# A PSUM copy at the head of the feed-forward unit: ScalarE moves h to SBUF, and the cubic, the square and the absolute value read the copy

## The chip, the cores and the metric

The kernel runs on one core of a Trainium2 chip. The metric is the device time of one execution in microseconds; of several runs the median counts. Engines are named as in the profile: PE is TensorE, DVE is VectorE, ACT is ScalarE, POOL is GpSimd, SP is SyncE (it issues DMAs).

## What is computed

Attention whose heads are mixed before and after the softmax, followed by a feed-forward part whose activation is a rational function. Cut to what matters here:

```python
# attention: 4 batches, 12 heads, 448 rows, 64 wide
scores = einsum('bhij,hg->bgij', q @ k.T / 8, w_pre)
attn   = einsum('bhij,hg->bgij', softmax(scores), w_post)
x      = (attn @ v)            # reshaped to 1792 tokens x 768

# feed-forward: 768 -> 2048 -> 768
h  = x @ w_in
P  = a[0] + a[1]*h + a[2]*h**2 + a[3]*h**3
Q  = 1 + abs(b[0])*abs(h) + abs(b[1])*h**2
out = (P / (Q + 1e-6)) @ w_out
```

## The kernel before

The program has two parts. The attention part goes over 16 tiles of query rows and takes roughly the first 350 us. The feed-forward part is 64 **units** (`put_unit(u)`), each 128 columns of the hidden width (of 2048) by one batch of 448 tokens; four units in a row have the same batch, and 16 such turns make up the whole. A matrix product is made in three passes from a high and a low part of each operand, so that a unit costs TensorE 36 matmuls of 448 columns: 18 for h (`m1`, L879) and 18 for the output (`m2`, L969, six groups of three, one for each 128 output columns).

A unit goes as follows. `m1` writes h into a bank of the PSUM tile `ps_s`, of which there are two. ACT reads the bank three times: `cubic` (L892, tile `m`), `square` (L895, tile `sq`) and `mag` (L898, tile `ua`); `den` (L902) makes the linear part of Q from the square. DVE reads the bank twice more: `horner1` (L905) and `horner2` (L908) multiply `m` by h. `den2` (L912) adds up Q, ACT takes `log` (L915) and `seed` (L919, an exponential) for a first reciprocal, DVE refines it (`step1` L922, `step2` L925) and forms the quotient (`quot` L929). `hi` rounds the result to the high part (L236 where ACT does it, L238 where DVE does), and `lo` (L939, POOL or DVE) subtracts for the low part. Both go into the tile `g`, which `m2` reads. The outputs of a turn are added to the partial sums on DVE (L1006) and leave by DMA.

In the same stretch the weights of the next turns are converted from 64-bit to a high and a low 32-bit part, in pieces of 384 columns (L410 ACT, L415 POOL, L419, L424 and L430 DVE, L236 ACT, L446 POOL); they share all three engines with the units until about 715 us.

The order of instructions on each engine is not that of the code. Every operation is entered in a plan with a guessed duration, a due time `at` and the operations that it must wait for. `Plan.run` then goes through time and writes an order for each engine; where an operation may run on either of two engines (`hi`, `lo`, some copies out of PSUM), it takes the first that is free. A `Ring` of n buffers makes the taker of buffer k wait for all uses of buffer k - n. The use that frees a bank of `ps_s` is set at the end of the unit's vector chain:

```python
o = add("pe", 18 * 0.204, m1, [w_ld[fi][0:4], *x_ld[xn], R["ps_s"].take(), m1_op.get(u - 1)], at=at, extra=0.1)
...
d1 = add("dve", 0.54, horner1, [a1, a2, a3], at=at)
d2 = add("dve", 0.6, horner2, [d1], at=at)
...
R["ps_s"].uses[-1].extend([a1, a2, a3, d2])
```

So `m1` of unit u + 2 waits for `horner2` of unit u, among others.

Of the kernel before, what the change touches and what calls it, by code (L numbers as in the profile page):

```python
# [9 lines left out]
F32 = mybir.dt.float32  # L10
# [8 lines left out]
B, H, S, D = 4, 12, 448, 64  # L19
# [35 lines left out]
class Plan:  # L55
# [11 lines left out]
    def add(self, eng, dur, fn, deps=(), at=0.0, extra=0.0, since=0.0, after=(), mode=None, late=0.0):  # L67
        op = Op(eng, dur, fn, [d for d in deps if d is not None], at, extra, since, mode, late)
        op.behind = list(after)
        self.ops.append(op)  # L70
        return op
# [107 lines left out]
class Ring:  # L179
# [5 lines left out]
    def take(self):  # L185

        k = len(self.uses)
        self.uses.append([])
        return Slot(self, k)


def act(n, sb=True):
    return 0.08 + 1.0e-3 * n + (0.05 if sb else 0.0)
# [40 lines left out]
def move(nc, eng, o, i):  # L234
    if eng is nc.scalar:
        eng.copy(o, i)  # L236
    else:
        eng.tensor_copy(o, i)  # L238
# [3 lines left out]
def mixed_attention_then_rational_ffn(ctx: ExitStack, tc, q, k, v, w, wmix, mask, a, b2, out):  # L242
# [3 lines left out]
    nc = tc.nc  # L246
# [5 lines left out]
    add = plan.add  # L252
# [6 lines left out]
    base, after = ctx.enter_context(ExitStack()), ctx.enter_context(ExitStack())  # L259
    left, right, pairs2 = ExitStack(), ExitStack(), ExitStack()  # L260
    sb = {}
# [7 lines left out]
    def open_pools(stack, side, sizes):  # L269
        for name, bufs in sizes:  # L270
            sb[name] = stack.enter_context(
                tc.tile_pool(name=name, bufs=bufs, side=side, reuse_waits="tile"))
# [4 lines left out]
    R = {n: Ring(i) for n, i in (  # L277
        ("d", 2), ("e", 6), ("st", 6), ("q", 3), ("k", 2), ("cr", 3), ("cm", 2), ("cg", 1),
        ("co", 2), ("ps_s", 2), ("ps_t", 2), ("ps_u", 2), ("ps_a", 2), ("a", 2), ("v", 2), ("xs", 1), ("xo", 3),
        ("t", 2), ("g", 3), ("x", 1))}  # L280

    kpre = const.tile([128, 64], F32, name="kpre")
    kpost = const.tile([128, 2, BT], F32, name="kpost")
# [16 lines left out]
    NR = 3  # L300
# [50 lines left out]
    b1_op = add("act", 0.4, fit_ab, [ab_ld], at=90.0, late=4.0)  # L351
# [446 lines left out]
    for i in range(len(VIA) * NCV):  # L798
        g = first[1] + 6 + (first[NT - 1] - first[1] - 3) * i // (len(VIA) * NCV)
# [2 lines left out]

    def begin():
        right.close()
        open_pools(after, "right", (("wr", NR), ("t", 2)))

    def rest():
        left.close()
# [57 lines left out]
    def put_unit(u):  # L866
# [3 lines left out]
        at = END1 + UNIT * u  # L870
        box = {}
# [13 lines left out]
        def new(nm):  # L885
            box[nm] = sb["t"].tile([128, S], F32, tag=nm, name=nm)
            return box[nm]

        def cubic():
            if u == 0:  # L890
                nc.scalar.preload_act_table_set("natural_log_exp_and_others")
            nc.scalar.activation(new("m"), box["h"], AF.Identity, scale=a_sb[:, 3:4], bias=a_sb[:, 2:3])  # L892

        def square():
# [46 lines left out]
        o = add("pe", 18 * 0.204, m1, [w_ld[fi][0:4], *x_ld[xn], R["ps_s"].take(), m1_op.get(u - 1)], at=at, extra=0.1)  # L941
        m1_op[u] = o
        w_use[fi].append(o)
        x_use[xn].append(o)
        t_free = R["t"].take()
        a1 = add("act", 0.61 if u else 1.9, cubic, [o, t_free, b1_op], at=at)
        a2 = add("act", act(S, False), square, [o, t_free], at=at)
        a3 = add("act", 0.52, mag, [o, t_free], at=at)
        a4 = add("act", 0.65, den, [a2, t_free, b1_op], at=at)
        d1 = add("dve", 0.54, horner1, [a1, a2, a3], at=at)  # L950
        d2 = add("dve", 0.6, horner2, [d1], at=at)
        d3 = add("dve", 0.54, den2, [a3, a4], at=at)
        a6 = add("act", act(S), log, [d3], at=at)
        a7 = add("act", act(S), seed, [a6, t_free], at=at)
        d4 = add("dve", 0.54, step1, [a7], at=at)
        d4 = add("dve", 0.6, step2, [d4], at=at)
        d5 = add("dve", 0.6, quot, [d4, d2], at=at)
        R["ps_s"].uses[-1].extend([a1, a2, a3, d2])
        a5 = add(copies(S, on=ON["g_hi"]), 0, hi, [d5, R["g"].take(), op_rest], at=at)
        d6 = add(subs(S, on=ON["g_lo"]), 0, lo, [a5], at=at)  # L960
        R["t"].uses[-1].append(d6)
# [149 lines left out]
```

## Time and profile before

| | |
|---|---|
| median of 3 runs | 845.81 us (841.18 to 846.6) |
| the profiled execution | 839.4 us |
| its span, first to last instruction | 837.6 us |
| granted TensorE clock, mean | 0.994 |
| busy share of the span | PE 96%, DVE 82%, ACT 59%, POOL 41% |

The profiled execution is one execution, and lies 1.8 us above its own span and 6.4 us under the median of the runs. Times inside it are read as differences and then set against the median. A busy PE is not PE at its peak, but idle time of PE is time in which it had nothing that it was allowed to start.

### The profile page before, as it was taken

The page shows a single profiled execution, that of the slowest core. Times are in us where ns is not written, and L with a number is a line of the kernel's source. Part 1 is how long each engine was busy: PE and PEld are TensorE (multiplying, and loading weights), DVE is VectorE, ACT ScalarE, POOL GpSimd, SP SyncE. Part 2 cuts the span into 40 slices and gives each one's busy share as a digit, 9 for nine tenths or more (in the row PEclk, how much of TensorE's full clock was granted, in tenths as well). Part 3 has the DMA queues.
Part 4 walks back from the last instruction along what each step waited for, and adds up shares of the span by engine and source line. Part 5 has one row for each costly group of instructions (what it writes and reads, how often), then busy time and mean ns, then how long its engine had stood idle before and what let it go on. Part 6 is the DMA issues. An engine that isn't in the chain of part 4 may idle for free.

```text
span 837.6 us, 23295 instructions
## 1 busy us (share of the span) xinstructions
PE 802.3 (96%) x9360; PEld 597.7 (71%) x9360; DVE 684.7 (82%) x1177; ACT 493.8 (59%) x1079; POOL 339.4 (41%) x464
## 2 busy tenths in 40 slices
PE   5789999999999999999999999999999999999998
PEld 1244454454444454589989899998999998999997
DVE  5677788788788888889988988999998999866665
ACT  2456667556565566576676665666566566445542
POOL 2224444343444343734555434465445455212111
PEclk8999999999999999999999999999999999999999
DMA  6678788677886775985633255753485544166314
GB/s 203 197 207 225 241 269 250 198 222 239 261 243 202 241 233 157 341 292 204 230 123 100 80 194 209 280 186 101 148 309 186 219 151 151 61 225 242 114 62 154
DMA packets 75355, 166.46 MB, mean 199 GB/s; under 512 B 12944, under 2 KB 52720, under 8 KB 74096
## 3 DMA queue, kind: packets, MB, share of 16 engines
q1 hardware_dynamic: 74648, 164.01, 59.1%
q8 instruction: 74, 1.21, 0.6%
q10 hardware_dynamic: 600, 0.97, 0.4%
q14 instruction: 33, 0.27, 0.1%
HBM read 88.50 MB, written 37.75 MB: 151 GB/s over the span
## 4 chain that ended last, share of the span: by engine, by line
PE 57%; DVE 16%; ACT 3%; issue 3%; POOL 2%; DMA 1%; SPq 0%; ACTq 0%; DVEq 0%; POOLq 0%
PE ps_s L879 19%; PE ps_u L969 6%; PE ps_a L969 6%; PE ps_t L969 6%; PE ps_a L640 5%; PE ps_s L496 5%; PE ps_t L565 3%; PE ps_u L705 3%; PE ps_u L565 2%; PE ps_t L705 2%; DVE cg L424 2%; DVE ua L925 2%; DVE cm L430 1%; DVE nm L571 1%; DVE ua L929 1%
## 5 line engine op out<-in xcount | busy, mean ns | idle before, releaser
L415 POOL TENSOR_SCALAR cm<-cm 128x384 f32<-128x384 f32 x64 | 103.3, 1616 | 46.6 <-ACT cm L410 46.3
L656 DVE STREAM_TRANSPOSE aa<-ps_a 128x448 f32<-128x448 f32 (+1 forms) x184 | 107.7, 617 | 13.7 <-PE ps_a L640 13.2
L939 POOL TENSOR_TENSOR g<-ua,g 128x448 fp32r<-128x448 f32 x47 | 57.8, 1230 | 138.8 <-ACT g L236 73.6
L600 POOL TENSOR_SCALAR krs<-kpost,rr 128x64 f32<-128x64 f32 x180 | 81.5, 466 | 74.3 <-DVE rr L591 54.0
L879 PE MATMUL ps_s<-xs,w 128*128 128x448 f32 x504 | 107.5, 366 | 2.9 <-DVE m L908 2.9
L879 PE MATMUL ps_s<-d,w 128*128 128x448 f32 x504 | 107.5, 366 | 1.3 <-DVE m L908 1.3
L496 PE MATMUL ps_s<-kk,q 64*64 64x448 f32 x720 | 94.4, 553 | 9.2 <-DMA kk<-in_k 5.0
L879 PEld LDWEIGHTS ps_s<-xs,w 128*128 128x128 f32 x504 | 94.4, 188 | 11.9 <-DVE m L908 4.0
L879 PEld LDWEIGHTS ps_s<-d,w 128*128 128x128 f32 x504 | 94.3, 188 | 10.3 <-DVE m L908 1.7
L236 ACT COPY st<-ps_s 120x448 f32<-120x448 f32 (+1 forms) x121 | 60.6, 533 | 68.1 <-PE ps_s L496 33.6
L640 PEld LDWEIGHTS ps_a<-e,krs 64*32 64x32 f32 x2880 | 45.2, 106 | 74.5 <-issue 34.4
L640 PE MATMUL ps_a<-e,krs 64*32 64x224 f32 x2880 | 93.6, 358 | 1.2 <-DVE aa L656 0.6
L446 POOL TENSOR_TENSOR w<-cm,w 128x384 fp32r<-128x384 f32 x48 | 54.7, 1140 | 87.7 <-ACT w L236 87.7
L892 ACT ACTIVATE m<-ps_s,a_sb 128x448 f32<-128x448 f32 x64 | 46.1, 720 | 69.5 <-PE ps_s L879 69.2
L969 PE MATMUL ps_u<-g,w 128*128 128x448 f32 x336 | 83.9, 366 | 0.0
L969 PE MATMUL ps_a<-g,w 128*128 128x448 f32 x336 | 83.8, 366 | 0.0
L969 PE MATMUL ps_t<-g,w 128*128 128x448 f32 x336 | 83.4, 366 | 0.0
L580 ACT ACTIVATE e<-ps_t,nm 128x448 f32<-128x448 f32 x92 | 57.7, 634 | 26.5 <-DVE nm L571 22.4
L587 POOL TENSOR_SCALAR sm<-sm 128x2 f32<-128x2 f32 (+1 forms) x92 | 20.9, 227 | 123.5 <-ACT e L580 121.4
L915 ACT ACTIVATE ua<-sq 128x448 f32<-128x448 f32 x64 | 37.0, 579 | 55.5 <-DVE sq L912 55.1
L580 ACT ACTIVATE e<-ps_u,nm 128x448 f32<-128x448 f32 x88 | 55.2, 634 | 24.0 <-DVE nm L571 20.4
L969 PEld LDWEIGHTS ps_t<-g,w 128*128 128x128 f32 x336 | 63.0, 188 | 5.6 <-DVE g L939 0.3
(89 smaller groups left out, 1516.5 us busy)
## 6 DMA issues: line engine op xcount, KB each, us to landing
d<-st SPq DMA_DIRECT2D x144, 210.0 KB
cr<-in_w SPq DMA_DIRECT2D x64, 384.0 KB
o_scr<-o SPq DMA_DIRECT2D x36, 448.0 KB
o<-o_scr SPq DMA_DIRECT2D x36, 448.0 KB
d<-x_scr SPq DMA_DIRECT2D x5, 2688.0 KB
xs<-x_scr SPq DMA_DIRECT2D x4, 2688.0 KB
d<-st SPq DMA_DIRECT2D x42, 157.5 KB
x_scr<-xs SPq DMA_DIRECT2D x12, 540.0 KB
```

The costliest lines, as they stand in the source:

```text
L236: eng.copy(o, i)
L415: nc.gpsimd.tensor_scalar(out=m, in0=m, scalar1=F64_MIN, scalar2=F64_MAX, op0=ALU.max, op1=ALU.min)
L446: eng.tensor_sub(t[:, 1, :], box["m"].bitcast(F32), t[:, 0, :].bitcast(F32))
L496: nc.tensor.matmul(box["s"][hh][i0:i1, 0:S], lhsT=Q[T][d, pr, i0:i1], rhs=K[b][d, pr, :], start=True, stop=True)
L580: nc.scalar.activation(e, box[r]["t"][:, 0:S], AF.Exp, bias=box[0]["nm"][:, r:r + 1], accum_out=box[0]["sm"][:, r:r + 1])
L600: eng.tensor_scalar_mul(box[r]["kr"], kpost, rr)
L640: nc.tensor.matmul(banks[c]["p"][q_:q_ + BT, JH * r:JH * (r + 1)], lhsT=box[r]["kr"][p, m_, :], rhs=box[r]["e"][p, JH * jh:JH * (jh + 1)], ...
L656: nc.vector.transpose(o, src)
L879: nc.tensor.matmul(h[:, 0:S], lhsT=W[fi][:, wi, kk * 128:(kk + 1) * 128], rhs=x[:, kk // 3, xj, kk % 3, :], start=(n == 0), stop=(n == 3 * ...
L892: nc.scalar.activation(new("m"), box["h"], AF.Identity, scale=a_sb[:, 3:4], bias=a_sb[:, 2:3])
L939: eng.tensor_sub(g[:, 1, :], box["rc"], g[:, 0, :].bitcast(F32))
L969: nc.tensor.matmul(O[key][:, 0:S], lhsT=W[fi][:, wi, DM + m * 128:DM + (m + 1) * 128], rhs=box["g"][:, gi, :], start=(f == 0 and n == 0), ...
```

## The change

ACT copies h out of the PSUM bank as the first step of a unit (`take`, L894, which calls the helper `move`, so that its rows have L236 or are told by their tile `h`). The copy lies in a new SBUF tile `h` with a single buffer. `cubic`, `square`, `mag`, `horner1` and `horner2` read the copy. The bank of `ps_s` is free once `take` is done; the single buffer `h` is free once `square`, `mag` and `horner2` of the unit are done, so that `take` of unit u + 1 waits for `horner2` of unit u. The plan's guessed costs for the three ACT operations are adjusted a little.

```diff
@@ rings and pools
-        ("t", 2), ("g", 3), ("x", 1))}
+        ("t", 2), ("h", 1), ("g", 3), ("x", 1))}
...
-        open_pools(after, "right", (("wr", NR), ("t", 2)))
+        open_pools(after, "right", (("wr", NR), ("t", 2), ("h", 1)))
@@ put_unit
-        def cubic():
+        def take():
             if u == 0:
                 nc.scalar.preload_act_table_set("natural_log_exp_and_others")
+            h = box["h"]
+            box["h"] = sb["h"].tile([128, S], F32, tag="h", name="h")
+            move(nc, nc.scalar, box["h"], h)
+
+        def cubic():
             nc.scalar.activation(new("m"), box["h"], AF.Identity, scale=a_sb[:, 3:4], bias=a_sb[:, 2:3])
...
-        a1 = add("act", 0.61 if u else 1.9, cubic, [o, t_free, b1_op], at=at)
-        a2 = add("act", act(S, False), square, [o, t_free], at=at)
-        a3 = add("act", 0.52, mag, [o, t_free], at=at)
+        a0 = add("act", act(S, False) + (0.0 if u else 1.3), take, [o, R["h"].take()], at=at)
+        R["ps_s"].uses[-1].append(a0)
+        a1 = add("act", 0.61, cubic, [a0, t_free, b1_op], at=at)
+        a2 = add("act", act(S), square, [a0, t_free], at=at)
+        a3 = add("act", 0.52, mag, [a0, t_free], at=at)
         a4 = add("act", 0.65, den, [a2, t_free, b1_op], at=at)
         d1 = add("dve", 0.54, horner1, [a1, a2, a3], at=at)
         d2 = add("dve", 0.6, horner2, [d1], at=at)
+        R["h"].uses[-1].extend([a2, a3, d2])
...
-        R["ps_s"].uses[-1].extend([a1, a2, a3, d2])
```

Since the plan sets the order, the change moves instructions, in the feed-forward part alone: the attention part up to the first units keeps its order. On PE the order is another one for the units 0 to 15, and the same as before from there on. On DVE and ACT rows move throughout. In the whole program DVE has 26 rounding casts of `hi` where it had 30, and 11 subtractions `lo` where it had 17 (the others are on ACT and POOL); of the units 16 to 48 alone these are 12 in place of 18, and 7 as before.

PE, around unit 12 (in the rows `ps_s` is written by `m1`, the other tiles by `m2`, x18 and x3 are matmuls in a row). Before, from the last piece of the outputs of unit 6 to the `m1` of unit 12, which is the third `m1` here:

```order
L969 MATMUL ps_a<-g,w_6258 128x448 x3
L969 MATMUL ps_a<-g,d 128x448 x3
L879 MATMUL ps_s<-d,w_6258 128x448 x18
L969 MATMUL ps_a<-g,d 128x448 x3
L879 MATMUL ps_s<-d 128x448 x18
L969 MATMUL ps_t<-g,w_6183 128x448 x3
L879 MATMUL ps_s<-xs,w_6183 128x448 x18
```

After, the `m1` of unit 11 and of unit 12 with what stands between them:

```order
L879 MATMUL ps_s<-d 128x448 x18
L976 MATMUL ps_u<-g,d 128x448 x3
L976 MATMUL ps_t<-g,w_6186 128x448 x3
L976 MATMUL ps_a<-g,d 128x448 x3
L976 MATMUL ps_t<-g,w_6186 128x448 x3
L976 MATMUL ps_a<-g,d 128x448 x3
L976 MATMUL ps_u<-g,w_6186 128x448 x3
L879 MATMUL ps_s<-xs,w_6186 128x448 x18
```

Before, three `m1` stand close together here, with one group of `m2` between each two of them; after, six groups of `m2` stand between two `m1`.

DVE, units 31 and 32 (`m` is written by `horner1`, TENSOR_TENSOR, and `horner2`; `sq` by `den2` and `step1`, `ua` by `step2` and `quot`; `cm` and `cg` are pieces of weights). Before, from `horner2` of unit 31:

```order
L908 SCALAR_TENSOR_TENSOR m<-m,a_sb,ps_s 128x448
L912 TENSOR_TENSOR sq<-sq,ua 128x448
L419 TENSOR_SCALAR cm<-cm 128x384
L424 SCALAR_TENSOR_TENSOR cg<-cr,cm 128x384
L905 TENSOR_TENSOR m<-m,ps_s 128x448
L430 SCALAR_TENSOR_TENSOR cm<-cr,cg 128x384
L908 SCALAR_TENSOR_TENSOR m<-m,a_sb,ps_s 128x448
L922 TENSOR_TENSOR sq<-sq,ua 128x448
L912 TENSOR_TENSOR sq<-sq,ua 128x448
L925 SCALAR_TENSOR_TENSOR ua<-sq,ua 128x448
L929 SCALAR_TENSOR_TENSOR ua<-m,a_sb,ua 128x448
```

After, from the same `horner2`:

```order
L913 SCALAR_TENSOR_TENSOR m<-m,a_sb,h 128x448
L419 TENSOR_SCALAR cm<-cm 128x384
L927 TENSOR_TENSOR sq<-sq,ua 128x448
L424 SCALAR_TENSOR_TENSOR cg<-cr,cm 128x384
L930 SCALAR_TENSOR_TENSOR ua<-sq,ua 128x448
L430 SCALAR_TENSOR_TENSOR cm<-cr,cg 128x384
L934 SCALAR_TENSOR_TENSOR ua<-m,a_sb,ua 128x448
L910 TENSOR_TENSOR m<-m,h 128x448
L917 TENSOR_TENSOR sq<-sq,ua 128x448
L913 SCALAR_TENSOR_TENSOR m<-m,a_sb,h 128x448
```

Before, `horner1` and `horner2` of unit 32 stand ahead of `step1`, `step2` and `quot` of unit 31; after, unit 31 is finished first.

ACT at the end of the program, units 62 and 63. Before, from `log` of unit 62:

```order
L915 ACTIVATE ua<-sq 128x448
L919 ACTIVATE ua<-ua 128x448
L892 ACTIVATE m<-ps_s,a_sb 128x448
L895 ACTIVATE sq<-ps_s 128x448
L898 ACTIVATE ua<-ps_s,b_sb 128x448
```

After, from the same `log`:

```order
L920 ACTIVATE ua<-sq 128x448
L236 COPY h<-ps_s 128x448
L924 ACTIVATE ua<-ua 128x448
L897 ACTIVATE m<-h,a_sb 128x448
L900 ACTIVATE sq<-h 128x448
L903 ACTIVATE ua<-h,b_sb 128x448
```

The copy of unit 63 stands between `log` and `seed` of unit 62, and `seed` waits behind it.

## Rows read from the trace of the kernel before

**Rows 1.** Busy time of each engine in five stretches of the span:

```profile
core 0: us, PE busy (x) PEld busy (x) DVE busy (x) ACT busy (x) POOL busy (x), PEclk, DMA share, GB/s
...
340.00:480.00 140.00, 137.35 (x1110) 119.62 (x1109) 124.79 (x215) 94.43 (x185) 69.46 (x70) 1.00 0.56 193
480.00:720.00 240.00, 237.62 (x1167) 218.75 (x1167) 219.52 (x358) 147.18 (x275) 118.66 (x89) 1.00 0.52 186
720.00:820.00 100.00, 100.00 (x495) 92.68 (x494) 67.72 (x114) 51.63 (x90) 15.58 (x14) 1.00 0.41 148
820.00:838.00 18.00, 13.66 (x68) 12.32 (x66) 8.61 (x15) 2.56 (x5) 2.49 (x2) 1.00 0.50 180
...
580.00:600.00 20.00, 18.66 (x92) 16.91 (x91) 19.46 (x31) 13.25 (x25) 11.20 (x8) 1.00 0.44 152
```

**Rows 2.** Waits of PE from 340 us on: total us, times, longest:

```profile
PE ps_s L879 <- DVE m L908: 4.2, 4, 1.6
```

**Rows 3.** Timeline at three of PE's four waits (brackets: idle before, releaser):

```profile
435.50 0.68 PE L879 MATMUL ps_s<-xs,w 128*128 128x448 f32 x2 [1.57 <-DVE m L908]
...
583.90 1.29 PE L879 MATMUL ps_s<-d,w 128*128 128x448 f32 x5 [1.33 <-DVE m L908]
...
702.59 1.69 PE L879 MATMUL ps_s<-xs,w 128*128 128x448 f32 x7 [1.05 <-DVE m L908]
```

**Rows 4.** ACT's and DVE's groups by form, 480 to 720 us:

```profile
L892 ACT ACTIVATE m<-ps_s,a_sb 128x448 f32<-128x448 f32 x33 | 23.8, 720 | 26.7 <-PE ps_s L879 26.7
L902 ACT ACTIVATE sq<-sq,c_sb,b_sb 128x448 f32<-128x448 f32 x33 | 25.2, 764 | 0.0
L895 ACT ACTIVATE sq<-ps_s 128x448 f32<-128x448 f32 x33 | 17.7, 535 | 0.0
L915 ACT ACTIVATE ua<-sq 128x448 f32<-128x448 f32 x32 | 18.5, 578 | 35.0 <-DVE sq L912 34.9
L908 DVE SCALAR_TENSOR_TENSOR m<-m,a_sb,ps_s 128x448 f32<-128x448 f32 x32 | 21.5, 671 | 0.1
L912 DVE TENSOR_TENSOR sq<-sq,ua 128x448 f32<-128x448 f32 x32 | 23.8, 745 | 0.0
L922 DVE TENSOR_TENSOR sq<-sq,ua 128x448 f32<-128x448 f32 x32 | 22.8, 714 | 7.0 <-ACT ua L919 6.7
L925 DVE SCALAR_TENSOR_TENSOR ua<-sq,ua 128x448 f32<-128x448 f32 x32 | 27.8, 870 | 0.6
L929 DVE SCALAR_TENSOR_TENSOR ua<-m,a_sb,ua 128x448 f32<-128x448 f32 x32 | 23.5, 734 | 0.6
L238 DVE CAST g<-ua 128x448 fp32r<-128x448 f32 x18 | 9.0, 500 | 1.8
```

**Rows 5.** Single lines, 480 to 720 us: ns shortest/median/longest:

```profile
L905 DVE TENSOR_TENSOR m<-m,ps_s x33: 605/611/622, 482.8 to 719.9; 128x448 f32<-128x448 f32 x33
L912 DVE TENSOR_TENSOR sq<-sq,ua x32: 607/616/1440, 483.4 to 712.3; 128x448 f32<-128x448 f32 x32
```

**Rows 6.** Timeline: `lo` on POOL, then the first `m2` of units 23, 31:

```profile
537.68 1.16 POOL L939 TENSOR_TENSOR g<-ua,g 128x448 fp32r<-128x448 f32 x1 [2.19 <-DVE g L238]
539.84 0.77 PE L969 MATMUL ps_t<-g,w 128*128 128x448 f32 x3
...
596.89 1.46 POOL L939 TENSOR_TENSOR g<-ua,g 128x448 fp32r<-128x448 f32 x1 [2.31 <-DVE g L238]
599.87 0.77 PE L969 MATMUL ps_t<-g,w 128*128 128x448 f32 x3
```

**Rows 7.** Timeline of the end, units 62 and 63:

```profile
818.51 0.73 ACT L892 ACTIVATE m<-ps_s,a_sb 128x448 f32<-128x448 f32 x1
...
822.60 0.58 ACT L915 ACTIVATE ua<-sq 128x448 f32<-128x448 f32 x1 [0.50 <-DVE sq L912]
...
826.55 1.15 POOL L939 TENSOR_TENSOR g<-ua,g 128x448 fp32r<-128x448 f32 x1 [2.96 <-DVE g L238]
...
828.03 0.77 PE L969 MATMUL ps_t<-g,w 128*128 128x448 f32 x3
```

## The prediction, written before the changed kernel was run

> **What bounds the kernel now.** I read the busy time by stretches first. From 340 us on the program is the feed-forward part, and PE is busy there all but a little: idle 2.65 us of 140, 2.38 of 240, none of 100, and 4.34 of the last 18 [rows 1]. The last of these is the closing sums and stores, which come behind the last matmul and which the change doesn't touch. So PE sets the time, at 36 matmuls a unit, and a change to the vector chain gains time only where PE waits for that chain. There is 2.65 + 2.38 = 5.0 us of idle time in front of the end, and nothing that this change does can gain more than that.
>
> The second view is what PE waits for. Of the 5.0 us, 4.2 us are four waits of `m1` for `horner2` [rows 2]: 1.57, 1.33 and 1.05 us [rows 3], which leaves 0.3 us for the fourth. It is the wait for a bank of `ps_s`: `m1` of unit u + 2 may start when `horner2` of unit u is done. That is the wait that the change loosens.
>
> The third view is the engine that is next. DVE is busy 219.5 of 240 us (91%) between 480 and 720 us, and 19.46 of 20 around the wait at 583.9 us [rows 1]. ACT has room there (147.2 of 240, 61%), and POOL (118.7, 49%). From 720 us on the weights are converted and DVE falls to 68 of 100. So the stretch where PE could be made to wait by a slower or later vector chain is 480 to 720 us, some 33 units.
>
> **What the change removes: the wait for the bank.** The bank is now free when the copy is done. The copy of unit u needs `m1` of u and `horner2` of u - 1, which comes some 7 us (a unit of PE's time: 240 us for 33 units [rows 1, 4]) before `horner2` of u. The three long waits were at most 1.57 us, so with 7 us of grace and 0.6 us of copy to pay, all four go. The gain is 4.2 us if nothing else is late in their place. The new order on PE for the units 0 to 15, which spreads the `m1` evenly, serves the same end: before, the 1.57 us wait came where the `m1` of units 10, 11 and 12 stood close together.
>
> **What it adds on ACT.** One copy a unit out of PSUM; the nearest row is `square`, which reads the same bank and writes SBUF: 0.535 us [rows 4]. The three readers change from PSUM to SBUF. `cubic` becomes what `den` is now, Identity with scale and bias out of SBUF: 0.764 in place of 0.720. `square` becomes what `log` is in size, 0.578 in place of 0.535 [rows 4], and `mag` I put up by the same 0.043. Together 0.535 + 0.044 + 2 x 0.043 = 0.67 us a unit, 22 us over 33 units; with six more rounding casts of some 0.57 us (0.535 and a little, estimated) it makes ACT 147 + 22 + 3.4 = 173 of 240 us, 72%. ACT hides it: it is idle while it waits for `m1` and for `den2` (26.7 and 34.9 us in [rows 4]). What isn't hidden is the length of a unit's chain, by the copy, a hand-over of 0.03 us and the slower reads: 0.70 us from `m1` to `horner1`.
>
> **What it does on DVE.** `horner1` and `horner2` now read two SBUF operands in place of one in PSUM and one in SBUF. That this may cost, two rows show. `horner1` never takes longer than 622 ns and never less than 605; `den2`, the same kind of operation with both operands in SBUF, takes 607 at least, 616 in the median, and up to 1440 [rows 5]. So there is no gain in the undisturbed duration, and a tail is added. The means of the four operations with both operands in SBUF lie over their floors: `den2` 745 and `step1` 714 against 612, `step2` 870 against 612, `quot` 734 against 671 [rows 4, 5], taking the floors from `horner1` and `horner2`. That is +0.13, +0.10, +0.26 and +0.06 us, 0.14 in the mean. The Trainium skill (SBUF — State Buffer, Who interferes with whom) says that a VectorE instruction with two SBUF inputs contends with a GpSimd instruction that reads SBUF, through a shared read port that the first to come holds. The spread in these rows agrees with that. For two operations I take 0.28 us a unit, with ends of 0.16 (2 x 0.08, the mean of the two smaller) and 0.39 (0.13 + 0.26): 33 units make 9.2 us, from 5.3 to 12.9. Against it, DVE has six casts fewer in the units 16 to 48, at 0.50 us [rows 4]: 3.0 us. Net +6.2 us, from 2.3 to 9.9, in a stretch where it had 240 - 219.5 = 20.5 us idle. DVE comes to 226 of 240, 94%.
>
> The Trainium skill (Perfetto Trace Analysis, Optimizing Scalar/DVE Operations) gives VectorE an access overhead of about 125 ns for PSUM against about 60 for SBUF, and by that the two operations would get cheaper by 0.13 us a unit, so that nothing is given back and the time is that of the full 4.2 us. Against it speak the shortest durations, 605 and 607 ns, which are the same [rows 5].
>
> **What is late next.** With the bank out of the way, the next thing that PE can wait for is `g`. In the stretch in question `lo` ends 1.0 us before the first `m2` of unit 23 starts (537.68 + 1.16 against 539.84) and 1.5 us before that of unit 31 (596.89 + 1.46 against 599.87) [rows 6]; three more units of the last place in their turn (35, 39, 47) are in the same position, and the other units of the stretch have more. Three things eat into it: the chain is 0.70 us longer, DVE is slower, and PE comes sooner by what it no longer waits (up to 2.4 us in this stretch). Against that the new order on DVE puts `step1`, `step2` and `quot` of unit 31 ahead of `horner1` and `horner2` of unit 32, at least 1.3 us (0.61 + 0.67 [rows 4, 5]) sooner. The two sides are about even. Ends: nothing is given back, or all that DVE gets more, 9.9 us, is passed on to PE. I take 1.2 us, half of the 2.4 us gained in this stretch, since 14 of DVE's 20.5 us of idle time are left to work a backlog off.
>
> **The end.** Unit 63 has 0.33 us to spare (826.55 + 1.15 = 827.70 against 828.03) [rows 7]. Worked through the new order with the prices above, one after the other: from 818.51 the copy 0.54, `seed` of unit 62 with 0.58 (as `log`), `cubic` 0.76, `square` 0.58 and `mag` 0.68 end at 821.65; then `horner1` and, now ahead of `horner2`, `den2` at 0.65 each, and a hand-over at either end, so that `log` starts at about 823.0 in place of 822.60 [rows 7]. That is 0.4 us, 0.1 more than the spare. Ends 0, where ACT's operations overlap, and 0.6 us (0.70 + 0.2 for DVE - 0.33), where the order gives nothing; I take 0.3.
>
> **The sum.** -4.2 + 1.2 + 0.3 = -2.7 us. Against the profiled execution of 839.4 us that is 836.7. That execution lies 6.4 us under the median, and no row says that the waits differ there; so against the median, 845.81 - 2.7 = 843.1, rounded to 843.0 us.
>
> **Rivals.** First, DVE takes it back and more. The place is 480 to 720 us. The price is two SBUF reads of 0.39 us a unit, 9.9 us net; it decides where the idle time of DVE is not where the backlog is, as around 583.9 us, where 0.54 of 20 us is idle [rows 1]. Then PE waits for `g` at the last units of the turns, and the sum is -4.2 + 9.9 + 0.3 = +6.0, 851.8 us; with the middle price, +6.2 in place of +9.9, it is +2.3, 848.1 us. For it speaks that DVE is at 97% there; against it, that PE had to wait only 2.4 us in 240 with this DVE.
>
> Second, the change doesn't free anything. The single buffer `h` makes `take` of unit u + 1 wait for `horner2` of u, and ACT executes in order: what stands behind `take` (`seed` of u in several places) waits too, and with it the chain that was to be freed. Where PE waited for `horner2`, it came up to 1.57 us after PE was free [rows 3]. Take 1.33 us, the wait at 583.9, as the delay of `seed`, and the longer chain of 0.70: with a spare of 1.0 us [rows 6], five units lose 5 x (1.33 + 0.70 - 1.0) = 5.2 us, and -4.2 + 5.2 + 0.3 = +1.3 makes 847.1 us. Against it: `horner2` stands within two DVE operations of `horner1` in nearly all units, and `log`, where it stands ahead of `take`, isn't held up.
>
> Third, all of the 4.2 us stay, and the end costs nothing: 841.6 us. It lies on the side of the forecast.
>
> **How the numbers follow.** The forecast with the third case, a gain of 1 to 4.2 us: 0.6. DVE takes it back: 0.25. Nothing is freed: 0.1. Something that I don't see: 0.05. The range takes in the third case and the first rival's middle price. The runs of before spread over 841.18 to 846.6, so 3 us are added at the low end and 2 at the high one: 838.5 to 850. One per cent, about what a measurement of this kernel can tell from no change, is 8.5 us. A gain of that size is more than the 5.0 us that PE idles, so 0.03; a loss of it needs more than the first rival's upper price, 0.06; within it 0.91.
>
> **What would show it.** PE's waits for `horner2` in front of `m1` are gone, all four. The copy takes about 0.54 us, `cubic` 0.76. `horner1` and `horner2` get a tail beyond 622 ns and means of some 0.7 to 0.85 us between 480 and 720 us, and DVE is busy 226 of 240 us. PE's waits there, if any, are for `g`, in the last units of turns, and sum to some 1 us. The prediction is wrong if PE's idle time between 340 and 820 us is over 5 us, or if the time changes by more than PE's idle time does, which would point to the attention part, whose order is the same.

## The result and the profile after

The changed kernel takes 854.39 us (median of 4 runs, 852.3 to 858.69), the kernel before in the same job 844.12 (4 runs, 841.18 to 846.6). The ratio is 1.0121, with a 95% interval of 1.0082 to 1.0159: the change costs some 10 us. 843.0 us was forecast, in a range up to 850; the time lies outside it, on the side of the first rival.

The profiled execution of after took 858.69 us, the longest of its four, and that of before, 839.4 us, lies below all of its runs. Part of the 19 us between the two is scatter ahead of the change: the first `m1` starts at 350.4 us in the one and 356.3 us in the other, though the attention part is the same, and in another execution of the kernel before it starts at 355.0 us. So the kernels are compared below by their medians and, of profiled executions, by the **feed-forward length**, from the start of the first `m1` to the end of the span: 487.2 us before, 487.1 in that other execution of it, 500.6 after. This length repeats far better than the whole.

Busy time by stretches of after, columns as in [rows 1]; the first row is the feed-forward part as a whole:

```profile
core 0: us, PE busy (x) PEld busy (x) DVE busy (x) ACT busy (x) POOL busy (x), PEclk, DMA share, GB/s
356.30:856.90 500.60, 485.96 (x2616) 439.81 (x2612) 420.98 (x668) 330.29 (x608) 225.85 (x159) 0.99 0.49 172
...
356.00:486.00 130.00, 125.63 (x884) 110.80 (x877) 107.07 (x174) 93.74 (x180) 68.86 (x54) 1.00 0.52 177
486.00:739.00 253.00, 246.35 (x1183) 223.80 (x1182) 231.84 (x363) 175.75 (x324) 138.29 (x92) 0.99 0.50 178
739.00:838.00 99.00, 99.00 (x490) 91.75 (x489) 71.33 (x116) 56.11 (x98) 16.54 (x14) 1.00 0.41 149
580.00:600.00 20.00, 16.55 (x72) 14.45 (x71) 18.25 (x29) 12.39 (x23) 10.48 (x9) 0.91 0.28 92
700.00:720.00 20.00, 17.54 (x78) 15.43 (x77) 18.21 (x29) 13.63 (x27) 10.67 (x8) 0.91 0.33 109
```

The same whole of before:

```profile
350.30:837.60 487.30, 479.12 (x2620) 438.06 (x2612) 410.73 (x680) 290.36 (x538) 198.67 (x155) 1.00 0.50 176
```

PE's idle time in the feed-forward part is 500.60 - 485.96 = 14.6 us where it was 487.30 - 479.12 = 8.2, so +6.5. Its busy time, for the same matmuls, is 486.0 in place of 479.1, so +6.8. The 13.3 us are in these two. Idle time is lost up to 739 us, while the weights are still converted (4.4 + 6.7 us against 5.0 in [rows 1]); behind that PE never stops for 99 us, as before. Of the longer busy time, most lies in two stretches of 20 us in which the granted clock has a mean of 0.91: PE is busy 16.55 and 17.54 us there with 72 and 78 matmuls, which at the rate of [rows 1] (495 in 100 us) would take 14.5 and 15.8, so 3.8 us more. Another part stands beside the waits, as time that the view counts as busy. An example, at a clock of 1.00:

```profile
520.51 0.37 PE L976 MATMUL ps_t<-g,w 128*128 128x448 f32 x1
521.29 0.67 PE L976 MATMUL ps_t<-g,w 128*128 128x448 f32 x2 [0.42 <-DVE g L944]
521.80 0.78 PE L976 MATMUL ps_u<-g,w 128*128 128x448 f32 x3
```

The first group of three takes 1.29 us from its start to that of the next, where groups start some 0.62 apart undisturbed; 0.42 of the 0.67 us between count as idle, 0.25 as busy. (Estimate: eight waits outside the two stretches, against four before, make some 1 us.) That leaves some 2 of the 6.8 us that no row here shares out.

What PE waits for in after, 340 us on (total us, times, longest):

```profile
PE ps_t L976 <- POOL g L944: 5.9, 8, 1.0
PE ps_t L976 <- ACT g L236: 3.9, 2, 2.4
...
PE ps_t L976 <- DVE g L238: 0.6, 1, 0.6
...
PE ps_t L976 <- DVE g L944: 0.4, 1, 0.4
```

The four waits for `horner2` in [rows 2] are gone, all of them. In their place are twelve waits for `g`, 10.8 us. The result of the vector chain comes too late for `m2`, at the first of its six groups. Counted by `quot`, 7.0 of the 10.8 us fall on the last units of turns (11, 19, 27 and 43), the rest on the units 10, 12 to 14 and 22; 3.3 us lie before 480 us.

DVE, POOL and ACT by form, 499 to 739 us of after (columns as in [rows 4]; `den2` is L917, `step1` L927, `step2` L930, `quot` L934):

```profile
L913 DVE SCALAR_TENSOR_TENSOR m<-m,a_sb,h 128x448 f32<-128x448 f32 x32 | 33.5, 1047 | 0.0
L917 DVE TENSOR_TENSOR sq<-sq,ua 128x448 f32<-128x448 f32 x32 | 24.8, 776 | 1.2 <-ACT sq L907 1.1
L927 DVE TENSOR_TENSOR sq<-sq,ua 128x448 f32<-128x448 f32 x32 | 24.6, 770 | 11.2 <-ACT ua L924 11.2
L930 DVE SCALAR_TENSOR_TENSOR ua<-sq,ua 128x448 f32<-128x448 f32 x32 | 22.6, 707 | 0.7
L934 DVE SCALAR_TENSOR_TENSOR ua<-m,a_sb,ua 128x448 f32<-128x448 f32 x32 | 22.4, 699 | 0.4
L910 DVE TENSOR_TENSOR m<-m,h 128x448 f32<-128x448 f32 x31 | 21.2, 682 | 0.7 <-ACT m L897 0.7
...
L446 POOL TENSOR_TENSOR w<-cm,w 128x384 fp32r<-128x384 f32 x27 | 37.7, 1400 | 26.5 <-ACT w L236 26.5
L944 POOL TENSOR_TENSOR g<-ua,g 128x448 fp32r<-128x448 f32 x25 | 36.5, 1461 | 49.2 <-DVE g L238 25.2 <-ACT g L236 24.0
...
L236 ACT COPY h<-ps_s 128x448 f32<-128x448 f32 x32 | 17.0, 530 | 17.2 <-DVE m L913 12.7 <-PE ps_s L879 2.4 <-DVE sq L927 1.7
```

`horner2` has a mean of 1,047 ns where it had 671 [rows 4], `horner1` 682 where its median was 611 [rows 5]. `step2` came down from 870 to 707: the six operations together go from 4.35 to 4.68 us a unit. POOL's subtractions are longer too: the low part of `g` took 1,229 ns in the mean in before (480 to 720 us), 1,461 now. The row of before, and that of the weights' low part in the second execution of before, 499 to 739 us:

```profile
L939 POOL TENSOR_TENSOR g<-ua,g 128x448 fp32r<-128x448 f32 x26 | 31.9, 1229 | 42.9 <-DVE g L238 24.6 <-ACT g L236 18.3
...
L446 POOL TENSOR_TENSOR w<-cm,w 128x384 fp32r<-128x384 f32 x26 | 29.3, 1128 | 48.6 <-ACT w L236 48.6
```

Single operations of after, same stretch (ns shortest/median/longest):

```profile
L913 DVE SCALAR_TENSOR_TENSOR m<-m,a_sb,h x32: 670/919/1595, 498.9 to 734.7; 128x448 f32<-128x448 f32 x32
...
L446 POOL TENSOR_TENSOR w<-cm,w x27: 1012/1398/2387, 507.1 to 733.7; 128x384 fp32r<-128x384 f32 x27
```

Sorted by what POOL does at the same time, over the whole feed-forward part of this trace: 39 of the 64 `horner2` overlap no subtraction of POOL and have a median of 675 ns; 22 overlap one by more than 0.3 us, and their median is 1,576.

The timeline around the longest wait of after:

```profile
568.47 1.32 POOL L446 TENSOR_TENSOR w<-cm,w 128x384 fp32r<-128x384 f32 x1 [1.04 <-ACT w L236]
...
568.84 1.43 DVE L913 SCALAR_TENSOR_TENSOR m<-m,a_sb,h 128x448 f32<-128x448 f32 x1
...
578.66 2.76 POOL L446 TENSOR_TENSOR w<-cm,w 128x384 fp32r<-128x384 f32 x2 [2.21 <-ACT w L236]
...
579.11 1.44 DVE L927 TENSOR_TENSOR sq<-sq,ua 128x448 f32<-128x448 f32 x1
...
580.59 1.32 DVE L930 SCALAR_TENSOR_TENSOR ua<-sq,ua 128x448 f32<-128x448 f32 x1
...
583.12 0.57 ACT L236 CAST g<-ua 128x448 fp32r<-128x448 f32 x1 [1.97 <-DVE ua L934]
...
583.74 0.47 PE L976 MATMUL ps_t<-g,w 128*128 128x448 f32 x1 [2.45 <-ACT g L236]
583.77 1.39 POOL L944 TENSOR_TENSOR g<-ua,g 128x448 fp32r<-128x448 f32 x1 [2.35 <-ACT g L236]
...
585.21 1.10 PE L976 MATMUL ps_t<-g,w 128*128 128x448 f32 x2 [1.00 <-POOL g L944]
...
586.11 1.32 PE L976 MATMUL ps_u<-g,w 128*128 128x448 f32 x3
...
587.23 1.32 PE L976 MATMUL ps_t<-g,w 128*128 128x448 f32 x3
...
589.11 0.78 PE L976 MATMUL ps_u<-g,w 128*128 128x448 f32 x3
589.73 0.78 PE L976 MATMUL ps_a<-g,w 128*128 128x448 f32 x3
```

In these rows the DVE operations on two SBUF tiles that lie beside a subtraction of POOL take about twice their time: `horner2` 1.43, `step1` 1.44, `step2` 1.32 us, against 0.6 to 0.7 undisturbed [rows 4, 5]; the subtractions take 1.3 to 1.4 us. PE stands still for 2.45 us and again for 1.00, and after that its groups of three matmuls start 1.12 us apart (586.11, 587.23) where they start 0.62 apart a little later (589.11, 589.73): the granted clock is at 1.2 GHz, the lower of its two levels, for a while, and at 2.4 GHz again afterwards. That is the 0.91 of the window above; two microseconds of it:

```profile
586.00:588.00 2.00, 2.00 (x7) 1.75 (x7) 1.97 (x5) 1.43 (x4) 0.79 (x1) 0.50 0.00 0
```

### The profile page after: what moved, and what is told of

Read it like the earlier page. It is cut to its first block, busy times and chain, and to the rows that moved or that the text cites. A ratio compares the mean times of both kernels' runs of the same rounds, so it can differ in the third digit from the quotient of the medians.

```text
span 856.9 us, 23412 instructions
## 1 busy us (share of the span) xinstructions
PE 815.0 (95%) x9360; PEld 600.2 (70%) x9360; DVE 695.7 (81%) x1165; ACT 534.0 (62%) x1149; POOL 366.6 (43%) x470
## 4 chain that ended last, share of the span: by engine, by line
PE 59%; DVE 20%; DMA 6%; ACT 6%; issue 5%; POOL 3%; SPq 1%; ACTq 0%; DVEq 0%; POOLq 0%
PE ps_s L879 16%; PE ps_s L496 7%; PE ps_a L640 6%; PE ps_u L976 6%; PE ps_t L976 6%; PE ps_a L976 5%; DMA d<-st 4%; PE ps_t L565 4%; PE ps_u L565 4%; ACT e L580 2%; PE ps_u L705 2%; PE ps_t L705 2%; DVE cg L424 2%; DVE ua L934 2%; DVE nm L571 2%
## 5 line engine op out<-in xcount | busy, mean ns | idle before, releaser
L944 POOL TENSOR_TENSOR g<-ua,g 128x448 fp32r<-128x448 f32 x53 | 73.8, 1393 | 160.4 <-DVE g L238 91.4
L415 POOL TENSOR_SCALAR cm<-cm 128x384 f32<-128x384 f32 x64 | 105.9, 1659 | 47.8 <-ACT cm L410 47.2
L236 ACT COPY st<-ps_s 120x448 f32<-120x448 f32 (+1 forms) x121 | 60.8, 533 | 76.3 <-PE ps_s L496 41.7
L496 PE MATMUL ps_s<-kk,q 64*64 64x448 f32 x720 | 97.0, 563 | 7.2 <-DMA kk<-in_k 5.2
L976 PE MATMUL ps_t<-g,w 128*128 128x448 f32 x336 | 88.3, 373 | 7.8 <-POOL g L944 4.2
L446 POOL TENSOR_TENSOR w<-cm,w 128x384 fp32r<-128x384 f32 x48 | 63.6, 1327 | 52.1 <-ACT w L236 52.1
L236 ACT COPY h<-ps_s 128x448 f32<-128x448 f32 x64 | 34.0, 532 | 65.4 <-PE ps_s L879 31.9
L927 DVE TENSOR_TENSOR sq<-sq,ua 128x448 f32<-128x448 f32 x64 | 47.3, 740 | 29.0 <-ACT ua L924 28.9
```

Of the source, the lines that this page charges most:

```text
L415: nc.gpsimd.tensor_scalar(out=m, in0=m, scalar1=F64_MIN, scalar2=F64_MAX, op0=ALU.max, op1=ALU.min)
L446: eng.tensor_sub(t[:, 1, :], box["m"].bitcast(F32), t[:, 0, :].bitcast(F32))
L496: nc.tensor.matmul(box["s"][hh][i0:i1, 0:S], lhsT=Q[T][d, pr, i0:i1], rhs=K[b][d, pr, :], start=True, stop=True)
L944: eng.tensor_sub(g[:, 1, :], box["rc"], g[:, 0, :].bitcast(F32))
L976: nc.tensor.matmul(O[key][:, 0:S], lhsT=W[fi][:, wi, DM + m * 128:DM + (m + 1) * 128], rhs=box["g"][:, gi, :], start=(f == 0 and n == 0), ...
```

## The experiments

The kernel before ran beside every group of them, at 843.0 to 844.9 us. "Feed-forward" is the feed-forward length of the profiled execution. (In e9, e10 and e12 POOL's results are left out, so that these three are compared with each other.)

| run | what is in it | median us | ratio to before, 95% | feed-forward us |
|---|---|---|---|---|
| before | | 844.12 | 1 | 487.2 |
| after | copy, five readers, 1 buffer, its own order | 854.39 | 1.008 to 1.016 | 500.6 |
| e1 | order of before; copy, five readers, 2 buffers | 857.25 | 1.008 to 1.022 | 499.0 |
| e2 | order of after, 2 buffers | 854.21 | 1.007 to 1.016 | 498.9 |
| e3 | order of after, horners read PSUM | 866.89 | 1.022 to 1.031 | 508.6 |
| e4 | 2 buffers known to the plan | 853.87 | 1.006 to 1.016 | 497.0 |
| e5 | order of before; copy, ACT's readers alone | 847.09 | 1.003 to 1.010 | 491.6 |
| e6 | order of before; only horners on SBUF | 851.01 | 1.006 to 1.012 | 495.2 |
| e7 | before once more | 843.20 | 0.996 to 1.000 | 487.1 |
| e8 | before, horners due earlier | 842.26 | 0.995 to 1.001 | 486.7 |
| e9 | before, POOL quiet | 836.97 | 0.991 to 0.996 | 481.3 |
| e10 | e1, POOL quiet | 839.28 | 0.993 to 0.998 | 481.3 |
| e12 | e5, POOL quiet | 839.23 | 0.993 to 0.998 | 481.7 |
| e11 | e4, measured DVE costs in the plan | 843.44 | 0.997 to 1.003 | 487.0 |
| e13 | after, measured DVE costs (1 buffer) | 849.48 | 1.004 to 1.013 | 495.1 |
| e14 | before, measured DVE costs | 839.51 | 0.993 to 0.999 | 482.4 |
| e15 | e4, guessed costs plus 5% | 850.50 | 1.006 to 1.012 | 491.2 |
| e16 | e4, measured costs less 10% | 843.46 | 1.000 to 1.005 | 487.9 |

**Is it the order, the buffer or the reads?** e1 keeps the plan and the order of before and puts the copy just ahead of `cubic`; the two buffers lie in a tile that is idle at that time.

```diff
+            h = box["h"]
+            box["h"] = sb["co"].tile([128, 2, CV], F32R, tag="co", name="h").rearrange("p a c -> p (a c)")[:, 0:S].bitcast(F32)
+            move(nc, nc.scalar, box["h"], h)
             nc.scalar.activation(new("m"), box["h"], AF.Identity, scale=a_sb[:, 3:4], bias=a_sb[:, 2:3])
```

> The plan and the order of the kernel before on every engine; the copy is issued just ahead of cubic, all five readers read it, and h has two buffers (in the space of the tile co, which is idle by then), so that nothing waits for horner2 but the second next copy. What is left of the change is the price of the operations: 0.7 us more on ACT's side of a unit's chain, and the two-SBUF reads of horner1 and horner2 on DVE. If the DVE reads are the cause, it loses most of the 10 us: 850 to 855 us. If the single buffer h or the new order is the cause, it comes out near the kernel before, 841 to 846 us, with PE's four waits for the bank gone or shorter.

It took 857.25 us. The loss is there without the new order. In the feed-forward part PE waits for `g` alone here, 10.5 us.

e2 is after with two buffers, the order untouched:

```diff
-            box["h"] = sb["h"].tile([128, S], F32, tag="h", name="h")
+            box["h"] = sb["co"].tile([128, 2, CV], F32R, tag="co", name="h").rearrange("p a c -> p (a c)")[:, 0:S].bitcast(F32)
```

> The order of the changed kernel on every engine, word for word, and all its reads; only h has two buffers, so that the copy of unit u + 1 no longer waits for horner2 of unit u. If the single buffer, by holding ACT's queue, is the cause: 843 to 847 us, and the 26 us in which the copy waited for horner2 between 356 and 740 us are gone. If the DVE reads or the new order are the cause: 851 to 855 us, as the changed kernel.

854.21 us. In after, `take` waits for `horner2` 30 times:

```profile
ACT h L236 <- DVE m L913: 29.2, 30, 3.0
```

In e2 that row is gone and the time is the same. e4 tells the plan of the second buffer (`("h", 2)` in the rings), which gives another order:

> The changed kernel with two buffers h, and the plan knows of them, so that the order is made anew. If the single buffer is the cause, 842 to 846 us, no slower than the run with two buffers in the unchanged order. If the DVE reads are, 850 to 855 us. If it is an order in which the first units run ahead and the outputs come late, anything between, and the first units tell.

853.87 us. With the plan's guessed costs a second buffer gives nothing back, in either order. (With other costs it does: e13 below.)

e3 is after with `horner1` and `horner2` reading the bank as before, the ACT readers on the copy:

```diff
-            h = box["h"]
+            h = box["hp"] = box["h"]
...
-            nc.vector.tensor_mul(box["m"], box["m"], box["h"])
+            nc.vector.tensor_mul(box["m"], box["m"], box["hp"])
...
-                out=box["m"], in0=box["m"], scalar=a_sb[:, 1:2], in1=box["h"], op0=ALU.add, op1=ALU.mult)
+                out=box["m"], in0=box["m"], scalar=a_sb[:, 1:2], in1=box["hp"], op0=ALU.add, op1=ALU.mult)
```

> The order of the changed kernel on every engine; horner1 and horner2 read the bank in PSUM as before, ACT's three readers read the copy. The copy's buffer is free after mag, so the wait of the copy for horner2 is gone too, and the bank is again held until horner2. If the DVE reads are the cause: 842 to 847 us, horner2 back from a mean of 1.05 us to 0.67. If the single buffer is: the same 842 to 847 us, but then the run with two buffers is as fast. If the order is: 851 to 855 us.

866.89 us, the slowest of all and above every value expected, with a new wait: in this order `m1` counts on a bank that is free early, and PE waits for `horner2` ten times, 15.9 us. It doesn't separate the reads from the order, so the next two go back to the order of before.

**The two halves alone.** e5 is e1 with the edit of e3: copy and ACT's readers, horners on PSUM.

> One half of the change in the order of the kernel before: ACT copies h just ahead of cubic, with two buffers, and cubic, square and mag read the copy; horner1 and horner2 read the bank in PSUM as before. It adds 0.7 us to the head of each unit's chain and to ACT, and nothing to DVE. If the DVE reads from SBUF are the cause: 844 to 848 us, since the longer head alone costs PE little. If ACT's added work and the longer chain are the cause: 851 to 857 us, as with all readers on the copy.

847.09 us, +3.6 over the before of its job (843.47) by the medians, 5.2 by the ratio of 1.0062. PE's waits are four for `horner2` as before, 6.4 us in place of 4.2: the chain is longer by the copy, and the bank comes free later. e1 and e5 differ only in where the two horners read h, and with it in when the bank is free: 857.25 against 847.09 us.

e6 has no copy; `horner1` and `horner2` multiply by a constant SBUF tile, so that the numerator of P/Q is not a function of h.

```diff
+    h_sb = const.tile([128, S], F32, name="h_sb")
...
+        nc.gpsimd.memset(h_sb, 0.5)
...
-            nc.vector.tensor_mul(box["m"], box["m"], box["h"])
+            nc.vector.tensor_mul(box["m"], box["m"], h_sb)
...
-                out=box["m"], in0=box["m"], scalar=a_sb[:, 1:2], in1=box["h"], op0=ALU.add, op1=ALU.mult)
+                out=box["m"], in0=box["m"], scalar=a_sb[:, 1:2], in1=h_sb, op0=ALU.add, op1=ALU.mult)
```

> The other half in the order of the kernel before: no copy, ACT's three readers read PSUM as before, and horner1 and horner2 read a constant tile in SBUF in place of the bank of h (so the numerator is not that of h). The bank is then free after mag, so that PE's waits for it go as well. If the DVE reads are the cause: 849 to 856 us, horner2 with a mean of 0.8 to 1.05 us. If ACT's side is: 840 to 843 us, the kernel before without its 4.2 us of waits.

851.01 us, +7.5, although `m1` no longer waits for `horner2`. 3.6 + 7.5 = 11.1 is near the loss of e1, 12.4, but it is no division of it: what PE waits for in e5 is the bank, which in e1 and e6 is free early. The forms of e6, 499 to 739 us:

```profile
L907 DVE TENSOR_TENSOR m<-m,h_sb 128x448 f32<-128x448 f32 x32 | 25.8, 806 | 0.0
L910 DVE SCALAR_TENSOR_TENSOR m<-m,a_sb,h_sb 128x448 f32<-128x448 f32 x31 | 25.4, 820 | 0.1
```

**Controls on before.** e7 is the kernel before once more; e8 makes `horner1` and `horner2` due 12 us earlier (`at=at - 12.0`), to free the bank by order.

> The kernel before once more, for a second profile of it: 841 to 847 us. The question is where the first unit's m1 starts. In the profile of before it starts at 350.4 us, in those of the changed kernel and three of its variants at 351.8 to 356.9. If that is scatter of the attention part, it lies anywhere from 350 to 357 us here too; if the change shifts the attention part, near 350.

> The kernel before, without a copy, but the plan gives horner1 and horner2 a due time 12 us earlier, so that DVE does them ahead of weights and sums that stand in front of them now. It goes after the same 4.2 us of waits for the bank without touching what is read where. If those waits are all that can be had: 840 to 845 us, PE's waits for horner2 under 2 us. If what is put behind comes late in its place: 845 to 849 us.

843.20 and 842.26 us: no difference, and in e8 the four waits stay, 4.0 us in all where under 2 were expected. This edit of the due times doesn't reach them.

**Is it the collision with POOL?** In e9 (before) and e10 (e1), POOL's three operations of the feed-forward part write without reading SBUF; the same edit is in e12 (e5).

```diff
-            nc.gpsimd.tensor_scalar(out=m, in0=m, scalar1=F64_MIN, scalar2=F64_MAX, op0=ALU.max, op1=ALU.min)
+            if g is None:
+                nc.gpsimd.memset(m, 1.0)
...
-            eng.tensor_sub(g[:, 1, :], box["rc"], g[:, 0, :].bitcast(F32))
+            if eng is nc.gpsimd:
+                eng.memset(g[:, 1, :].bitcast(F32), 0.0)
```

> The kernel before in its own order, with POOL quiet in the feed-forward part: its three operations there (clamp of the weights' low word, low part of the weights, low part of g) are memsets, which write the same tiles and read nothing from SBUF. Left out of the computation: those three results. This is the base for the next two runs. If POOL's reads and DVE's two-operand SBUF reads slow each other, DVE's den2, step1, step2 and quot fall to their floors (means 745, 714, 870, 734 ns to at most 640, 640, 690, 690), DVE is busy some 15 us less of the 240 between 499 and 739 us, and the time is 836 to 843 us, since PE had only 5 us to gain. If these means are the operations' own, they stay, and the time is 840 to 844 by POOL's shorter operations alone. If a memset's writes disturb DVE as the reads did, the means stay too.

> The same quiet POOL (the same three results left out) with the copy in the order of before, all five readers on the copy, two buffers h: e1 with POOL quiet. Theory (the two horner reads cost time because POOL reads SBUF at the same time): horner1 and horner2 fall from means of 777 and 863 ns to at most 640 and 700, and the run is at most 4 us above the run before it in this list (what ACT's copy and the longer chain cost, 3.6 us at a noisy POOL). Rival (two SBUF operands or DVE's load as such): the run stays 8 to 13 us above it. If the chain's length alone does it, this run and the next differ by nothing and both stand 3 to 4 us above the base.

> The same quiet POOL (the same three results left out), order of before, ACT's copy and its three readers on the copy, horner1 and horner2 on PSUM: e5 with POOL quiet. It splits the run before it: contention expects the same time within 2 us, and both 0 to 4 us above the base; the rival expects this one 6 us or more below the run with all readers on the copy.

836.97, 839.28 and 839.23 us. In e9, without any copy, `den2`, `step1`, `step2` and `quot` come down from 745, 714, 870 and 734 ns [rows 4] to 618, 619, 621 and 681, and PE doesn't wait between 499 and 739 us. `step2` of e9:

```profile
L931 DVE SCALAR_TENSOR_TENSOR ua<-sq,ua 128x448 f32<-128x448 f32 x33 | 20.5, 621 | 0.6
```

The two horner operations of e10, with both operands in SBUF, against the same rows of e1 (499 to 739 us); e1:

```profile
L911 DVE SCALAR_TENSOR_TENSOR m<-m,a_sb,h 128x448 f32<-128x448 f32 x31 | 26.8, 863 | 0.1
L908 DVE TENSOR_TENSOR m<-m,h 128x448 f32<-128x448 f32 x32 | 24.9, 777 | 0.0
```

e10:

```profile
L917 DVE SCALAR_TENSOR_TENSOR m<-m,a_sb,h 128x448 f32<-128x448 f32 x33 | 22.4, 677 | 0.1
L914 DVE TENSOR_TENSOR m<-m,h 128x448 f32<-128x448 f32 x33 | 20.4, 618 | 0.7 <-ACT m L901 0.6
...
L949 POOL MEMSET g<- 128x448 f32 x27 | 13.4, 497 | 53.7 <-PE ps_a L981 43.7 <-issue 8.7 <-DVE sq L921 1.3
```

e12, on PSUM:

```profile
L917 DVE SCALAR_TENSOR_TENSOR m<-m,a_sb,ps_s 128x448 f32<-128x448 f32 x33 | 22.2, 673 | 0.1
...
L914 DVE TENSOR_TENSOR m<-m,ps_s 128x448 f32<-128x448 f32 x33 | 20.2, 612 | 0.7 <-ACT m L901 0.5
```

The extra time is gone, to 618 and 677 ns, where e12 has 612 and 673 on PSUM. So two SBUF operands cost next to nothing by themselves; POOL's reads at the same time do. The time bears it out: moving the horners to SBUF costs some 9 us beside POOL's subtractions (e1 loses 12.4 us, e5 3.6, each against the before of its job) and nothing beside its memsets (e10 = e12, feed-forward 481.3 and 481.7), with a reservation: the memset needs no finished `hi`, so that the chain is also shorter by the subtraction of POOL, and these three kernels have more slack than the real ones.

**Or is it the plan?** e11 was meant to show that no order takes this time away. It is e4 with the measured means in the plan:

```diff
-        d1 = add("dve", 0.54, horner1, [a1, a2, a3], at=at)
-        d2 = add("dve", 0.6, horner2, [d1], at=at)
+        d1 = add("dve", 0.68, horner1, [a1, a2, a3], at=at)
+        d2 = add("dve", 1.0, horner2, [d1], at=at)
...
-        d3 = add("dve", 0.54, den2, [a3, a4], at=at)
+        d3 = add("dve", 0.74, den2, [a3, a4], at=at)
...
-        d4 = add("dve", 0.54, step1, [a7], at=at)
-        d4 = add("dve", 0.6, step2, [d4], at=at)
-        d5 = add("dve", 0.6, quot, [d4, d2], at=at)
+        d4 = add("dve", 0.76, step1, [a7], at=at)
+        d4 = add("dve", 0.72, step2, [d4], at=at)
+        d5 = add("dve", 0.72, quot, [d4, d2], at=at)
```

> The changed kernel with two buffers h known to the plan, and the plan's costs of the six DVE operations of a unit set to the means measured after the change (horner1 0.68, horner2 1.0, den2 0.74, step1 0.76, step2 0.72, quot 0.72 us). If the loss is DVE's and POOL's extra time, which no order takes away, 849 to 856 us, as with the guessed costs (853.9). If it is a wrong order, because the plan thinks DVE faster than it is, 842 to 847.

843.44 us: the theory fell. Feed-forward is 487.0 us, the same as before. Its row from 499 to 739 us and PE's waits from 340 us on:

```profile
499.00:739.00 240.00, 237.89 (x1167) 218.22 (x1166) 230.24 (x352) 167.15 (x311) 124.20 (x83) 1.00 0.53 189
```

```profile
PE ps_t L976 <- POOL g L944: 2.3, 3, 1.2
PE ps_t L976 <- DVE o L1013: 1.3, 1, 1.3
...
PE ps_s L879 <- ACT h L236: 0.3, 1, 0.3
```

The same stretch in after:

```profile
499.00:739.00 240.00, 233.35 (x1120) 211.91 (x1119) 220.40 (x344) 165.79 (x306) 131.12 (x87) 0.99 0.52 184
```

DVE is fuller than in after, 230 against 220 of 240 us, the collisions are still there (`horner2` 982 ns in the mean), and PE waits 3.9 us in place of 10.8. Four more runs ask whether that order was only lucky; the cost changes are of the same form.

> The changed kernel as it is, one buffer h, with the plan's six DVE costs at the measured means (as e11, which had two buffers and came to 843.4). Theory (the order counts on a DVE that is too fast): 842 to 847. If the second buffer was needed for that, 849 to 855: take waits for horner2 (29 us in the changed kernel) and what stands behind it on ACT waits too. If e11 was a lucky order, anywhere from 843 to 856.

> The kernel before, with no copy, and the plan's six DVE costs at the means of its own trace (horner1 0.61, horner2 0.67, den2 0.75, step1 0.71, step2 0.87, quot 0.73 us). PE idled 5.0 us between 340 and 820 us before, 4.2 of them for horner2. Theory: the order of before had little to lose, so 838.5 to 843, at most 4.5 us better; then the copy costs 0 to 5 us between two orders made alike. Rival (orders scatter whatever the costs): up to 850.

> The control for luck: the changed kernel with two buffers h, the plan's guessed costs of the six DVE operations raised by 5% only (0.567 and 0.63 us). The order is another one in hundreds of places, and DVE still counted too fast by 0.6 us a unit. Theory: it stays with the guessed costs, 850 to 857. If orders scatter whatever the costs, it may as well be 843.

> The other side of the control: two buffers h, the measured costs less 10% (0.61, 0.90, 0.67, 0.68, 0.65, 0.65 us). Another order again, close to the true costs. Theory: 842 to 848, near e11's 843.4. If orders scatter whatever the costs, it may as well be 854.

849.48, 839.51, 850.50 and 843.46 us. With two buffers, the two orders from costs near the measured ones come to 843.4 and 843.5, the two from costs near the guesses to 853.9 and 850.5. That speaks against scatter; it is four orders of many, and doesn't rule it out. With one buffer the measured costs are not enough: e13 stays 6 us above e11 (`take` waits for `horner2` 32 times, 33.8 us), and its interval overlaps that of after. So of the 10 us of the changed kernel the second buffer alone gives back nothing (e2), the measured costs alone at most some 5 (e13), and both together all (e11, e16). And before gains too, 843.0 to 839.5, ratio 0.993 to 0.999, with no wait of PE for `horner2` left: e14 is the fastest kernel here that computes everything. Between orders made alike, copy and reads cost 3.9 us with two buffers (e14 to e11; 4.6 of feed-forward length), and 10.0 with the single buffer of the change (e14 to e13).

## Why the prediction was wrong, step by step

- **The wait that goes.** Right: -4.2 us of waits for `horner2`, all four.
- **ACT.** The prices were right (copy 0.530 us against 0.535; ACT 166 of 240 us against 173 forecast). What the longer chain costs in the changed kernel no run separates: the 3.6 us of e5 are waits for a bank that the change frees early, and with POOL quiet it is 0.4 us of feed-forward length, 2.3 by the medians (e9 to e12).
- **DVE.** The tails were read rightly: e9 takes them away. The price was mis-sized. The two reads were put at +0.28 us a unit, at most 0.39; they cost 0.07 + 0.38 = 0.45. Their models were the tails of `den2`, `step1`, `step2` and `quot`, +0.26 at most; `horner2` got a longer one. But the other four operations came down by 0.11, which leaves +0.33 a unit, inside the ends, and DVE was busy 220 of 240 us, not the 226 forecast. So the sum of DVE's work is not what failed. What POOL loses by the same collision (0.23 us a piece for the low part of `g`, which lies on the chain) was in no term.
- **What is late next.** This is the step that failed. 1.2 us were to be given back to PE, "since 14 of DVE's 20.5 us of idle time are left to work a backlog off". It was 10.8 us of waits for `g`, and the lower clock behind the longest of them. The reason was wrong too, and e11 shows it: PE waits less with a DVE that idles less. Idle time in the sum of a stretch did not work the backlog off in an order that was fixed beforehand from 0.54 and 0.60 us, for operations that now take 0.68 and 1.05. With the measured costs and a second buffer the same reads cost nothing against before (e11), and 3.9 us against before with its own measured costs (e14). The end of the range, "all that DVE gets more, 9.9 us, is passed on to PE", was nearer.
- **The time and the idle time.** Both signs of being wrong came true: PE idles 12.5 us between 340 and 820 us (busy 467.5 of 480), and the time changes by more than the idle time does. The second was to point to the attention part. It didn't: the surplus is PE's longer busy time in the feed-forward part, 3.8 of the 6.8 us at the lower clock, and the sum had no term for it.
- **The end.** 0.3 us were put there; PE is busy without a stop from 739 to 838 us, and none of the twelve waits comes after 708 us. Nothing is lost there.
- **The rivals.** The first, DVE takes it back and more, had the mechanism and, for 7.0 of the 10.8 us, the units; that its 851.8 us came near is in part luck, since it had neither the lower clock nor POOL's loss. A chance of 0.25 was too little. The second, the single buffer, costs nothing in the order as it was made (e2), but in an order from the measured costs it keeps 6 us (e13), so that the measured costs alone don't take the loss away. That the price of the new reads depends on the plan's costs was in none of them.

The Trainium skill (SBUF — State Buffer, Who interferes with whom) says that a VectorE instruction with two SBUF inputs contends with a GpSimd instruction that reads SBUF and not with one that only writes it. e1 and e10 agree: 777 and 863 ns beside reads, 618 and 677 beside memsets. The lower access price for SBUF that the Trainium skill gives VectorE (Perfetto Trace Analysis, Optimizing Scalar/DVE Operations) isn't there in these operations: 618 and 677 ns on SBUF in e10 against 612 and 673 on PSUM in e12.

What stays open: which share of the 10 us the collisions would have with a plan that sees them one by one, why the single buffer and the guessed costs each hide what the other costs, and where the last 2 us of PE's longer busy time lie.

## What to carry to other kernels

Before a PSUM operand of a VectorE operation is moved to SBUF, look at what GpSimd reads at the same time: here a second SBUF operand was all but free beside memsets (618 and 677 ns against 612 and 673), and beside subtractions single operations took more than twice their shortest time on both engines (670 to 1,595 ns on VectorE, 1,012 to 2,387 on GpSimd). Idle time of an engine, summed over a stretch, was no cover here, where the order of its work is fixed from guessed durations; ask what the order believes of the operation that gets longer. When a change alters durations under a planner, put the measured ones into the plan of both kernels before the two are compared: here that was 10 us for the copy with two buffers and 3.5 for the kernel before, and between the two it leaves 4 us; with the single buffer of the change it leaves 10.

## What the runs showed of the hardware that was not expected

- The collision is paid on both sides: POOL's low part of the weights goes from 1,128 to 1,400 ns in the mean, that of `g` from 1,229 to 1,461, while `horner2` goes from 671 to 1,047.
- A wait of PE costs more than its length: behind the idle 2.45 and 1.00 us at 583.7 us the groups of three matmuls came 1.12 us apart in place of 0.62 until 588 us, and the mean granted clock of the 20 us was 0.91. Before, the wait of 1.33 us at about the same time [rows 3] left it at 1.00 [rows 1], and so did four waits of 0.58 to 0.87 us between 460 and 480 us of after.
- The start of the first `m1` wanders between 350.4 and 362.6 us in kernels whose edits all lie in the feed-forward part (350.4 in before and e13, 362.6 in e14), while the feed-forward length of two executions of before agrees to 0.1 us.
